# Head of a fused layernorm, linear attention and gated MLP kernel: one warm matmul fewer, an ungated load, one copy on another engine, one tile's statistics moved

## The chip, the cores and the metric

One core of a Trainium2 chip. The metric is device time in microseconds of one execution, the median of five runs. The engines named here are TensorE (PE, with PEld for its weight loads), VectorE (DVE), ScalarE (ACT), GpSimd (POOL) and SyncE (SP, which only issues transfers here). Each of them runs its own list of instructions in order and waits on semaphores for the others.

## What is computed

```python
xn = _layernorm(x)                        # x: 1 x 2048 x 448, bf16
# A: linear attention, 16 heads of 28
qkv = (xn @ wqkv)                         # wqkv: 448 x 1344
pq, pk = phi(q), phi(k)                   # phi(t) = where(t > 0, t + 1, exp(t)) + 1e-6
kv = einsum("bhsd,bhse->bhde", pk, v)
z = einsum("bhsd->bhd", pk)
s = ((pq @ kv) / (pq . z + 1e-6)) @ wo
# B: squared-ReLU MLP with a gate
h = relu(xn @ w1 + b1) ** 2               # w1: 448 x 1792
g = silu(h @ w2 + b2)
return x + s * g
```

All inputs and the output are bfloat16.

## The kernel before

The 2048 tokens are cut into 16 tiles of 128, four tiles to a group. Every tile is loaded token by token (`x_tok`), normalized (`xn`) and transposed (`xT`, features on the partitions), because the matmuls contract over features. The 448 features are three chunks of 128 and one of 64; the last 64 stand twice in `xn` (the "twin" copy, line 496), so that the remainders of two products can run side by side in the two halves of the array.

The kernel is written as a list of operations (`Op`) that a small planner in `Program` puts in order. `add` (line 64) notes what an operation reads and writes. `schedule` (line 87) lays the operations out on an estimated time line and so fixes the order on each engine; TensorE and SyncE keep the order in which the code adds their operations, while the other engines take the ready operation with the least `late`, for which `prio` stands in where it is set. `after` holds an operation back until others are placed. `emit` (line 227) writes each engine's list with the semaphore waits that remain. Every DMA has a semaphore of its own, and each engine one counter.

The change touches the head, in which tiles 0 to 3 go through by hand:

- Loads: tile 0 by SyncE (line 436), tile 1 by ScalarE's queue (437), tiles 2 and 3 by SyncE (439), b1 by ScalarE's queue (440), weights by SyncE. The load of tile 1 names `ones`, a small constant that POOL sets (line 374), as something it reads, so it waits for that memset.
- `warm(n, wide=True)` (line 1036) adds n matmuls of 128x512 on constant data into an unused bank, ahead of all others on TensorE.
- For each tile: statistics (`st`, 458) and their aggregate (`mv`, 459) on VectorE; Ln and Exp (`ln`, 468; `ex`, 472) on ScalarE give the reciprocal standard deviation; VectorE writes xn (`xn`, 481), in two parts for tiles 0 and 1, and the twin (`xd`, 496).
- `pe_transpose` (line 501) adds transposes on TensorE (510) and one copy from PSUM to `xT`, on VectorE (520) or ScalarE (521). Tiles 0 and 1 are transposed in two halves of two chunks: `turn(si, part, eng)`.
- Between them stand the K matmuls of tiles 0 and 1 (621, in the order of lines 1063 to 1069), the transpose of b1 and its copy (1072, 1074), and the matmuls of the first four rows of `w_1` (668, `h_mains`). `rests` (line 587) closes them with the 64-row remainders.
- The order on VectorE and ScalarE is written out by name in lines 1089 to 1096: each name waits in the plan for all names ahead of it in its list.

After the head the groups follow as streams of K, Q and H products (lines 1112 to 1140), then the token sums, the folding of the weights, and the last products with the output (lines 1141 to 1194). None of this is touched. The lists of instructions differ on TensorE, VectorE, ScalarE and POOL only where the section on the change says; SyncE's is the same.

## Time and profile before

| | |
|---|---|
| median of 5 runs | 142.04 us (141.97 to 142.19) |
| the profiled execution | 142.07 us, span 140.8 us |
| TensorE busy | 137.4 us (98%), 1225 matmuls |
| VectorE busy | 92.0 us (65%) |
| ScalarE busy | 78.6 us (56%) |
| GpSimd busy | 22.9 us (16%) |
| warm matmuls, line 1042 | 10, first at 0.84 us |
| landing of x tiles 0, 1 | 2.3 us, 2.5 us after issue |
| landing of x tiles 2 and 3 | 4.1 us after issue |

The span runs from the first to the last instruction that the profiler recorded; the time of the execution holds 1.27 us more. A row of the timeline gives start, duration, engine, line, operation, result and operands, how many instructions it merges, and in brackets the idle time of the engine ahead of it with what ended it. Durations of matmuls include the way through the array, so that neighbours overlap; the pace is read from the distance of their starts.

### The profile page before, as it was taken

Reading aid. Unit: us, or ns where it says so; the run is one execution under the profiler, and the core shown is the slowest. Engines: PE = TensorE matmul, PEld = TensorE weight load, DVE = VectorE, ACT = ScalarE, POOL = GpSimd, SP = SyncE. Lnnn points to the kernel's source line nnn. Section 1 sums busy time; section 2 is a strip of 40 time slices with the busy share of each in tenths; the row PEclk is TensorE's granted clock in tenths of the full one; section 3 lists DMA queues with packets and bytes.
Section 4 is the critical chain, followed back from the end, with each engine's and each line's share of the span. In section 5 each row is a group of like instructions: output and inputs, shape, how many; then the busy total and the mean of one; then the engine's idle time right before and its main releaser. Section 6 shows DMA issues by size and latency. Waiting matters only on the chain.

```text
span 140.8 us, 3056 instructions
## 1 busy us (share of the span) xinstructions
PE 137.4 (98%) x1225; PEld 68.3 (49%) x1225; DVE 92.0 (65%) x224; ACT 78.6 (56%) x152; POOL 22.9 (16%) x38
## 2 busy tenths in 40 slices
PE   7999999999999999999999999999999999999992
PEld 2365444444444444444455445644555555555482
DVE  1989888898878997779959910228936072442753
ACT  3668787978888896979799561523033030300220
POOL 6000000000000000000770000000001419092670
PEclk9999999999999999999999999999999999999999
DMA  4999266999822400000000035980000202122022
GB/s 121 291 304 262 61 169 119 367 294 183 141 41 49 84 14 0 0 19 5 0 0 0 5 81 151 196 167 4 5 0 0 70 0 95 35 69 66 33 96 74
DMA packets 20210, 12.91 MB, mean 92 GB/s; under 512 B 9380, under 2 KB 19812, under 8 KB 20196
## 3 DMA queue, kind: packets, MB, share of 16 engines
q1 hardware_dynamic: 18188, 11.45, 32.7%
q10 hardware_dynamic: 2008, 1.27, 4.0%
q8 instruction: 10, 0.16, 0.5%
q14 instruction: 4, 0.03, 0.1%
HBM read 8.78 MB, written 2.10 MB: 77 GB/s over the span
## 4 chain that ended last, share of the span: by engine, by line
PE 98%; DVE 0%; issue 0%; DVEq 0%
PE pb L935 30%; PE pb L668 30%; PE pb L621 9%; PE pb L1001 8%; PE pb L702 7%; PE pb L652 6%; PE pb L1042 3%; PE pb L708 1%; PE pb L510 1%; PE pb L795 1%; PE pb L756 1%; PE pb L833 0%; DVE xn L971 0%; PE pb L826 0%; DVE xn L980 0%; PE pb L791 0%
## 5 line engine op out<-in xcount | busy, mean ns | idle before, releaser
L668 PE MATMUL pb<-xT,w 64*128 64x512 bf16 (+2 forms) x408 | 51.3, 365 | 0.0
L935 PE MATMUL pb<-w,r 64*128 64x448 bf16 (+3 forms) x378 | 44.7, 343 | 0.0
L677 ACT ACTIVATE r<-pb,b1f 128x512 bf16<-128x512 f32 x56 | 34.9, 689 | 2.8 <-PE pb L668 2.8
L668 PEld LDWEIGHTS pb<-xT,w 64*128 64x128 bf16 (+1 forms) x408 | 22.8, 94 | 22.1 <-ACT r L677 0.5
L935 PEld LDWEIGHTS pb<-w,r 64*128 64x128 bf16 (+1 forms) x378 | 22.7, 95 | 20.0 <-issue 1.2
L911 ACT ACTIVATE gbuf<-gbuf 128x448 bf16<-128x448 bf16 (+1 forms) x16 | 8.7, 565 | 36.0 <-DVE gbuf L946 34.3
L946 DVE TENSOR_TENSOR gbuf<-pb,b2b 128x448 bf16<-128x448 f32 (+1 forms) x16 | 9.3, 609 | 29.2 <-PE pb L935 29.2
L980 POOL TENSOR_TENSOR xn<-xn,x_tok 128x448 bf16<-128x448 bf16 x15 | 15.0, 1031 | 48.8 <-DVE xn L971 48.8
L621 PE MATMUL pb<-w_qkv,xT 64*128 64x512 bf16 (+1 forms) x106 | 17.7, 377 | 0.0
L652 PE MATMUL pb<-xT,w_qkv 64*128 64x512 bf16 x84 | 15.5, 376 | 0.0
L685 DVE TENSOR_TENSOR r<-r 128x512 bf16<-128x512 bf16 x39 | 13.5, 419 | 0.0
L385 POOL MEMSET kvm<- 128x2048 bf16 x1 | 1.8, 1804 | 64.0 <-DVE zb L646 64.0
L458 DVE BATCH_NORM_STATS2 st<-x_tok 128x6 f32<-128x448 bf16 x16 | 9.3, 612 | 3.1 <-DMA x_tok<-in_A_x_dram 3.1
L599 ACT ACTIVATE qk<-pb 128x512 bf16<-128x512 f32 x16 | 8.9, 595 | 4.1 <-PE pb L621 3.6
L609 DVE SCALAR_TENSOR_TENSOR qk<-pb,qk 128x512 bf16<-128x512 f32 x16 | 10.7, 687 | 0.3
L1001 PE MATMUL pb<-msb,pqT 64*128 64x448 bf16 (+3 forms) x93 | 10.9, 343 | 0.0
L971 DVE TENSOR_TENSOR xn<-pb,gbuf 128x448 bf16<-128x448 f32 (+2 forms) x17 | 9.2, 591 | 2.0 <-ACT gbuf L911 1.5
L686 ACT ACTIVATE r<-r 128x512 bf16<-128x512 bf16 x17 | 9.7, 651 | 0.0
L621 PEld LDWEIGHTS pb<-w_qkv,xT 64*128 64x128 bf16 (+1 forms) x106 | 6.6, 94 | 6.3 <-DVE xT L520 0.4
L702 PE MATMUL pb<-qk,xn 128*128 128x448 bf16 x48 | 9.4, 352 | 0.0
L599 ACT ACTIVATE pqT<-pb 128x512 bf16<-128x512 f32 x12 | 6.8, 597 | 3.2 <-PE pb L668 1.6
L652 PEld LDWEIGHTS pb<-xT,w_qkv 64*128 64x128 bf16 x84 | 6.0, 94 | 5.0
(77 smaller groups left out, 98.7 us busy)
## 6 DMA issues: line engine op xcount, KB each, us to landing
out_dram<-xn SPq DMA_DIRECT2D x15, 112.0 KB, 1.7
w<-in_B_w_dram SPq DMA_DIRECT2D x1, 1568.0 KB, 10.0
x_tok<-in_A_x_dram SPq DMA_DIRECT2D x3, 448.0 KB, 3.6
xT<-rows ACTq DMA_DIRECT2D x6, 112.0 KB
w<-in_B_w_dram SPq DMA_DIRECT2D x1, 576.0 KB, 5.2
xT<-rows SPq DMA_DIRECT2D x5, 112.0 KB
w_o<-in_A_wo_dram SPq DMA_DIRECT2D x1, 392.0 KB, 11.2
w_qkv<-in_A_wqkv_dram SPq DMA_DIRECT2D x1, 384.0 KB, 3.4
```

Source lines behind the costliest of these rows:

```text
L599: add("act", lambda e, _: e.activation(out=slot, in_=src(), func=AF.Exp), [buf, "actw"], [tile], 0.6)
L609: lambda e, _: e.scalar_tensor_tensor(out=slot, in0=src(), scalar=1.0 + 1e-6, in1=slot, op0=ALU.add, op1=ALU.max),
L621: return e.matmul(ps(b)[:, 0:512], xT[half[h], c, si * P : (si + 1) * P], w_qkv[half[h], c, 384 : 2 * D], start=start, stop=stop,)
L652: return e.matmul(ps(b)[:, 0:512], w_qkv[half[h], c, m * P : (m + 1) * P], xT[half[h], c, g * 512 : (g + 1) * 512], start=start, stop=stop,)
L668: return e.matmul(ps(b)[:, c0 : c0 + n], w_1[half[h], c, fi * P : (fi + 1) * P], xT[half[h], c, t : t + n], start=start, stop=stop,)
L677: lambda e, _: e.activation(out=slot, in_=ps(b)[:, 0:512], func=AF.Relu, bias=b1f[:, fi : fi + 1]),
L685: return e.tensor_tensor(out=slot, in0=slot, in1=slot, op=ALU.mult)
L686: return e.activation(out=slot, in_=slot, func=AF.Square)
L702: last = e.matmul(ps(b)[:, 0:D], xn[:, si, c * P : (c + 1) * P], pk_of(si), start=(si == 0), stop=(si == NT - 1),)
L935: return e.matmul(ps(b)[:, 0:n], r2[half[h], fi, si * P : (si + 1) * P], w_2[half[h], fi, c], start=start, stop=stop)
L980: eng, lambda e, _: e.tensor_tensor(out=ob, in0=ob, in1=x_tok[:, si, c], op=ALU.add),
L1001: return e.matmul(ps(b)[:, 0:n], q, m, start=start, stop=stop)
```

## The change

Four edits, all in the head:

- nine warm matmuls instead of ten
- the load of x tile 1 no longer names `ones`, so it waits for nothing
- the copy of the second half of tile 1's transpose goes from VectorE to ScalarE, where it stands behind the copy of the first half and ahead of Ln and Exp of tile 2
- on VectorE the statistics and aggregate of tile 3 follow those of tile 2 directly

```diff
-        load_x(1, 2, "act", ["ones"]).prio = -118
+        load_x(1, 2, "act").prio = -118
...
-        warm(10, wide=True)
+        warm(9, wide=True)
...
-        turn(1, 1, "dve")
+        turn(1, 1, "act")
...
-            ("dve", "st0 mv0 st1 mv1 xn00 xn01 xd0 xn10 xn11 xd1 st2 mv2 xT11 st3 mv3 xn2 xd2 xn3 xd3 xT3"),
-            ("act", "ln0 ex0 ln1 ex1 xT00 xT01 xT10 ln2 ex2 b1 ln3 ex3 xT2"),
+            ("dve", "st0 mv0 st1 mv1 xn00 xn01 xd0 xn10 xn11 xd1 st2 mv2 st3 mv3 xn2 xd2 xn3 xd3 xT3"),
+            ("act", "ln0 ex0 ln1 ex1 xT00 xT01 xT10 xT11 ln2 ex2 b1 ln3 ex3 xT2"),
```

In the lists that come out, one of the ten matmuls of line 1042 is gone from TensorE, and its third K matmul of tile 1 waits for ScalarE instead of VectorE. One copy of line 520 is gone from VectorE, and there is one more of line 521 on ScalarE. On POOL the planner now puts the memset of `ones` behind those of `b1r`, `eps5` and `ident`, and the memset of `eps6` behind the selection that makes `ident`. The banks of PSUM are the same.

## The prediction

> **What bounds the kernel now.** First the page: its own time, the chain that ended last, and the tensor engine's share.

> ```profile
> span 140.8 us, 3056 instructions
> ...
> PE 98%; DVE 0%; issue 0%; DVEq 0%
> ```

> The chain is the tensor engine's own work from end to end, and this profiled execution took 142.07 us, 1.27 more than its span. The list of waits says where that engine stands still. For matmuls between 9.7 us and the end it names none; for weight loads it names a few of 0.3 to 0.4 us, which lie under running matmuls. So only the head counts, the first 9.6 us, in which tiles 0 to 3 are normalized and transposed. There the waits name two releasers:

> ```profile
> PEld pb L510 <- DVE xn L481: 1.2, 4, 0.6
> PEld pb L621 <- DVE xT L520: 0.4, 1, 0.4
> ```

> Then the timeline of the head, engine by engine (start, us, what, idle before). TensorE, where PEld is the weight load that shows when a matmul was released:

> ```profile
> 0.84 4.43 PE L1042 MATMUL pb<-const-bfloat16-1.0 128*128 128x512 bf16 x10 [0.84 <-PEq L1210]
> 5.00 0.55 PEld L510 LDWEIGHTS pb<-ident,xn 128*128 128x128 bf16 x4 [0.64 <-DVE xn L481]
> 5.71 0.11 PEld L510 LDWEIGHTS pb<-ident,xn 128*128 128x128 bf16 x2 [0.16 <-DVE xn L481]
> 6.41 1.08 PE L621 MATMUL pb<-w_qkv,xT 128*128 128x512 bf16 x4
> 7.09 0.10 PEld L621 LDWEIGHTS pb<-w_qkv,xT 128*128 128x128 bf16 x1 [0.37 <-DVE xT L520]
> 8.12 0.31 PEld L510 LDWEIGHTS pb<-ident,xn 128*128 128x128 bf16 x4 [0.21 <-DVE xn L481]
> 8.84 0.31 PEld L510 LDWEIGHTS pb<-ident,xn 128*128 128x128 bf16 x4 [0.22 <-DVE xn L481]
> 9.54 0.10 PEld L621 LDWEIGHTS pb<-w_qkv,xT 64*128 64x128 bf16 x2 [0.21 <-issue]
> ```

> VectorE, which works almost without a pause from 3.14 to 9.0:

> ```profile
> 3.14 0.63 DVE L458 BATCH_NORM_STATS2 st<-x_tok 128x6 f32<-128x448 bf16 x1 [3.14 <-DMA x_tok<-in_A_x_dram]
> ...
> 3.90 0.59 DVE L458 BATCH_NORM_STATS2 st<-x_tok 128x6 f32<-128x448 bf16 x1
> ...
> 6.78 0.26 DVE L520 COPY xT<-pb 128x256 bf16<-128x256 bf16 x1
> 6.95 0.62 DVE L458 BATCH_NORM_STATS2 st<-x_tok 128x6 f32<-128x448 bf16 x1
> 7.61 0.18 DVE L459 BATCH_NORM_AGGREGATE mv<-st 128x2 f32<-128x6 f32 x1
> 7.70 0.36 DVE L481 TENSOR_SCALAR xn<-x_tok,mv,rstd 128x448 bf16<-128x448 bf16 x1
> ```

> ScalarE and its queue:

> ```profile
> 0.93 0.40 ACTq L396 DMA_DIRECT2D x_tok<-in_A_x_dram  x1
> ...
> 5.41 1.01 ACT L521 ACTIVATE xT<-pb 128x256 bf16<-128x256 bf16 x3
> 6.90 0.29 ACT L468 ACTIVATE vep<-mv,eps 128x1 f32<-128x1 f32 x1 [0.48 <-DVE mv L459]
> ...
> 7.82 0.29 ACT L468 ACTIVATE vep<-mv,eps 128x1 f32<-128x1 f32 x1
> ```

> To be seen: each transpose waits for VectorE's normalized tile, VectorE's row is set by the landing of x tile 0 at 3.14, and the stalls of the matmuls after 5.85 are small. From the starts of single matmuls: 0.04 before the one released at 7.09, 0.09 and 0.04 around the transposes at 8.12, 0.10 and 0.04 around those at 8.84, 0.31 together. The 0.10 at 9.54 follows the switch to 64-row tiles; later switches (70.5, 95.3) cost the same, so no edit touches it.

> **The change, part by part.** *The tenth warm matmul.* It begins at 4.63 and takes 0.43, so the array is free at 5.06. The weights of the first transpose are in at 5.00, released by xn of tile 0. Without the tenth, that transpose starts at 5.01, 0.05 earlier. It doesn't last: the fifth transpose, at 5.72, waits for tile 1's xn (the row 5.71), which VectorE's order sets, and the K matmuls at 5.85 stand behind it. Bounds 0.00 to 0.05; I take 0.00, since the row 5.71 is the nearest. What the nine do to the clock is the first rival.

> *x tile 1 at once.* Its DMA leaves ScalarE at 0.93 after the memset of `ones`; SyncE's first DMA leaves at 0.81, so it comes forward by at most 0.12. Gain: none. Tile 1's statistics start at 3.90, straight behind tile 0's aggregate, without a wait for data. The b1 transfer behind it on that queue moves too; its reader at 7.32 waits for nothing. On POOL the `ones` memset goes back past three others (0.1 to 0.2 us each) and the memsets of b1r, eps5 and ident come forward a few hundredths; `ident` was ready at 1.73 for a use at 5.00, `ones` is read near 79 us. SyncE's queue is unchanged. Price: tile 1's packets meet tile 0's. Between 1.8 and 2.4 us the queue view has 73 packets, all SyncE's; between 2.4 and 2.8 it has 97 of ScalarE's and 77 of SyncE's at a DMA share of 1. A start that is 0.12 earlier can push tile 0's landing by 0 to 0.12; I take 0.05, since tile 0 had over half its packets through before tile 1's first. All of VectorE's row moves with it.

> [...]

> *xT of tile 1, second half, on ScalarE.* Its transposes end near 6.57. VectorE began the copy at 6.78, behind tile 2's statistics, and ended at 7.04. ScalarE is free at 6.42; it took up its first copy 0.03 after the transposes (5.41), so it starts here at 6.60 and, at 0.38 (first of the three at 5.41), ends at 6.98. The K matmul waiting at 7.09 had its place at 7.06: 0.04 gained. Behind the copy on ScalarE stands tile 2's Ln, at 6.90 now: copies follow each other at 0.31, so it starts between 6.91 and 7.01, Exp 0.32 later, Exp's end 0.20 after that: 7.43 to 7.53, and xn of tile 2 0.04 to 0.08 later (as for tiles 3 and 0): 7.47 to 7.61.

> *Tile 3's statistics moved up.* They start at 6.78 instead of 6.95; the aggregate goes from 7.61 to 7.44 and leaves VectorE free for xn of tile 2 at 7.53 instead of 7.70. With ScalarE's bound that is 7.53 to 7.61, so 0.09 to 0.17 gained; tile 2's transposes come at 8.00 to 8.04 instead of 8.13, since the matmuls before them end no earlier than 8.00. For tile 3 the Ln at 7.82 had waited for the aggregate's end at 7.79. Now that end is 7.62, but the b1 copy (7.58, now 7.54, 0.18 long) is ahead on ScalarE: Ln at 7.65 to 7.75, 0.07 to 0.17 earlier. Exp, xn, the transposes at 8.84 and the matmuls behind them follow by the same amount. These transposes are the head's last wait, so 0.07 to 0.17 goes on to the end; I take the middle, 0.12. Next late is nothing on record: matmuls never wait after 9.7, and the four copies and statistics that follow move along.

> Sum: 0.00 + 0.12 − 0.05 = 0.07 gained. On the profiled execution's 142.07 that gives 142.00; the median of the runs is 0.03 below it, so **141.97**. Ends: 0.17 gained with no delay, 141.87; 0.07 gained with 0.12 of delay, 142.09.

> **Rivals.** *The clock opens late (slower).* Warm matmuls are loaded every 0.43 us; the four of L621 after 6.41 take 0.22 each. The trace's clock record grants full speed from 5.13, 4.29 us after the first warm matmul, and takes it back at 141.66, 3.4 us after the last matmul's end near 138.3. So the gate judges stretches of some 3.4 us. In the one that ended at 5.13 the tensor engine was full; with nine it is idle from 4.63 to 5.01. If that share no longer suffices, the next chance comes near 8.53. Then from 5.85 on: two matmuls 0.86, two transposes 0.21, four matmuls 1.71, to 8.63; from there at full speed, b1 and six matmuls 0.71, transposes and matmuls of tiles 2 and 3 with nothing left to wait for 1.10, the switch 0.10: 10.54 instead of 9.55, less 0.04 for the matmul in which the clock opens. That is 0.95 more, **142.99**. For it: the idle stretch is new, the work after it is short transposes. Against: nine still fill nine tenths of the stretch, and the times of before lie within 0.22 us, so no run there missed its opening, wherever the stretch began. It decides if the K matmuls come 0.43 apart. Its bounds are 0 and, cold until 9.55, some 2.9 (3.2 of work doubled, less 0.31 of stalls).

> [...]

> *The early transfer eats the gain.* Tile 0 lands 0.12 or more late: 142.05 to 142.12. For it: every later start on VectorE hangs on 3.14. Against: over half of tile 0 is through by then.

> *All stalls go.* If Ln of tile 3 slips ahead with the statistics and the copies overlap as well as the first three did, all 0.31 goes: **141.73**. For it: VectorE loses 0.26 of work between 6.0 and 9.0. Against: the b1 copy and its transpose hold ScalarE.

> **How the numbers follow.** My forecast 0.45; late clock 0.27; transfer eats it 0.13; all stalls go 0.13; something else 0.02. Under 0.2% (0.28 us) a measurement here can hardly be told from no change. Faster by more: the case of all stalls and a little besides, 0.15. Slower: the late clock and the rest, 0.29. Within: 0.56. The likeliest case's own range is 141.87 to 142.09. To leave out under 2 in 10 the range has to reach down to the full gain and up through most of the late clock: 141.70 to 143.05.

> **What would show it.** Right: statistics of tile 0 at 3.14 to 3.26; first transpose near 5.0, fifth at 5.7 to 5.8; the copy of tile 1 on ScalarE near 6.6; the K matmul without a stall; tile 2's transposes at 8.0 to 8.1 and the first 64-row matmul at 9.4 to 9.5. Wrong: L621 matmuls at 0.43 each after 5.85, a start of VectorE past 3.3, or Exp of tile 2 later than 7.6.

## The result and the profile after

| | before | changed |
|---|---|---|
| median | 142.16 us (80 runs, 141.97 to 143.28) | 142.39 us (45 runs, 142.04 to 145.0) |
| ratio to before | | 1.0026, 95% interval 1.0016 to 1.0037 |
| profiled execution | 142.07 us, span 140.8 | 142.17 us, span 140.8 |

A little slower, and the table's last row doesn't show it: the two profiled executions have the same span. The difference is in the spread. Each run has a time and a span (first to last recorded instruction). In 134 runs of the kernel before that were taken beside the experiments, the mean time is 142.23, the mean span 140.99, and time less span is never over 1.30. In the 45 runs of the changed kernel the means are 142.64 and 141.18. They include its longest run, 145.0, which the ratio leaves out as over 1.5% above the fastest. So of 0.41 us in the mean, 0.20 lies in the span and 0.21 outside it (0.35, 0.14 and 0.21 without the longest run):

- 9 of the 45 spans are at 141.7 us or more (141.8 to 143.8), against 2 of 134 before.
- 20 of the 45 runs have more than 1.30 us outside the span (1.35 to 2.44).
- The 14 runs that have neither and a span of at most 141.1 average 142.13; the like runs of before 142.16.

So the undisturbed run is where the forecast put it, on the level of before or a little under; what costs is two kinds of disturbance, spans that are longer and time outside the span.

First the page of the changed kernel: its span, the instruction fetches of queue q8, read as the tensor engine's (packets, MB, share), and the chain that ended last.

```profile
span 140.8 us, 3054 instructions
...
q8 instruction: 9, 0.15, 0.4%
...
PE 95%; DMA 2%; DVE 2%; issue 0%; DVEq 0%
```

The chain now begins with the landing of x tile 0 and VectorE's first instructions: the warm matmuls no longer reach up to the first transpose. Two instructions fewer are in the span, a weight load and its matmul, and q8 has 9 packets where the page of before has

```profile
q8 instruction: 10, 0.16, 0.5%
```

Then the head of the changed kernel, TensorE's weight loads (start, us, what, idle before):

```profile
5.17 0.55 PEld L510 LDWEIGHTS pb<-ident,xn 128*128 128x128 bf16 x4 [1.24 <-DVE xn L481]
...
7.18 0.10 PEld L621 LDWEIGHTS pb<-w_qkv,xT 128*128 128x128 bf16 x1 [0.32 <-ACT xT L521]
...
8.81 0.31 PEld L510 LDWEIGHTS pb<-ident,xn 128*128 128x128 bf16 x4 [0.22 <-DVE xn L481]
...
9.52 0.10 PEld L621 LDWEIGHTS pb<-w_qkv,xT 64*128 64x128 bf16 x2 [0.21 <-issue]
```

VectorE:

```profile
3.31 0.63 DVE L458 BATCH_NORM_STATS2 st<-x_tok 128x6 f32<-128x448 bf16 x1 [3.31 <-DMA x_tok<-in_A_x_dram]
...
6.95 0.59 DVE L458 BATCH_NORM_STATS2 st<-x_tok 128x6 f32<-128x448 bf16 x1
7.57 0.18 DVE L459 BATCH_NORM_AGGREGATE mv<-st 128x2 f32<-128x6 f32 x1
7.67 0.37 DVE L481 TENSOR_SCALAR xn<-x_tok,mv,rstd 128x448 bf16<-128x448 bf16 x1
```

and ScalarE:

```profile
0.83 0.40 ACTq L396 DMA_DIRECT2D x_tok<-in_A_x_dram  x1
...
6.75 0.38 ACT L521 ACTIVATE xT<-pb 128x256 bf16<-128x256 bf16 x1 [0.16 <-PE pb L510]
7.06 0.29 ACT L468 ACTIVATE vep<-mv,eps 128x1 f32<-128x1 f32 x1
7.39 0.20 ACT L472 ACTIVATE rstd<-vep 128x1 f32<-128x1 f32 x1
7.67 0.18 ACT L1074 ACTIVATE b1f<-pb 128x14 f32<-128x14 bf16 x1
7.79 0.29 ACT L468 ACTIVATE vep<-mv,eps 128x1 f32<-128x1 f32 x1
```

Tile 0's statistics begin at 3.31 instead of 3.14, 0.17 later, and yet the first 64-row matmul comes at 9.52 instead of 9.54: the copy and the statistics gave 0.2 back on the way.

### The profile page after: what moved, and what is told of

Read it like the earlier page. It is cut to its first block, busy times and chain, and to the rows that moved or that the text cites. A ratio compares the mean times of both kernels' runs of the same rounds, so it can differ in the third digit from the quotient of the medians.

```text
span 140.8 us, 3054 instructions
## 1 busy us (share of the span) xinstructions
PE 136.7 (97%) x1224; PEld 68.3 (49%) x1224; DVE 91.8 (65%) x223; ACT 79.1 (56%) x153; POOL 22.9 (16%) x38
## 3 DMA queue, kind: packets, MB, share of 16 engines
q10 hardware_dynamic: 2008, 1.27, 3.5%
## 4 chain that ended last, share of the span: by engine, by line
PE 95%; DMA 2%; DVE 2%; issue 0%; DVEq 0%
PE pb L935 30%; PE pb L668 30%; PE pb L621 9%; PE pb L1001 8%; PE pb L702 7%; PE pb L652 6%; DMA x_tok<-in_A_x_dram 2%; PE pb L510 1%; PE pb L708 1%; DVE st L458 1%; PE pb L795 1%; PE pb L756 1%; PE pb L833 0%; DVE xn L971 0%; DVE mv L459 0%; PE pb L826 0%
## 5 line engine op out<-in xcount | busy, mean ns | idle before, releaser
L621 PE MATMUL pb<-w_qkv,xT 64*128 64x512 bf16 (+1 forms) x106 | 17.7, 377 | 0.0
L458 DVE BATCH_NORM_STATS2 st<-x_tok 128x6 f32<-128x448 bf16 x16 | 9.3, 610 | 3.8 <-DMA x_tok<-in_A_x_dram 3.8
L621 PEld LDWEIGHTS pb<-w_qkv,xT 64*128 64x128 bf16 (+1 forms) x106 | 6.7, 94 | 6.2 <-ACT xT L521 0.3
```

Of the source, the lines that this page charges most:

```text
L458: add("dve", lambda e, _: e.bn_stats(st6[:, si, :], x_tok[:, si, :]), [("x", si)], [("st", si)], 0.58),
L621: return e.matmul(ps(b)[:, 0:512], xT[half[h], c, si * P : (si + 1) * P], w_qkv[half[h], c, 384 : 2 * D], start=start, stop=stop,)
```

## The experiments

Spans and times are of all runs of a kernel (11 or 12 each), beside the kernel before on the same chip. "Start" is the start of tile 0's statistics and "head" the first 64-row matmul, both of the profiled execution.

| | start | head | mean span (before) | spans ≥ 141.7 | outside > 1.30 |
|---|---|---|---|---|---|
| e1 nine alone | 3.15 | 9.55 | 141.11 (140.94) | 1 of 12 | 7 of 12 |
| e2 ungated alone | 3.30 | 9.70 | 141.22 (140.94) | 1 of 11 | 0 |
| e3 order alone | 3.25 | 9.45 | 140.81 (140.94) | 0 | 0 |
| e4 the change with ten | 3.29 | 9.49 | 140.90 (140.94) | 0 | 0 |
| e5 nine, count kept | 3.20 | 9.60 | 140.86 (140.98) | 0 | 0 |
| e6 ten, a pair less at the end | 3.26 | 9.67 | 140.88 (140.98) | 1 of 12 | 1 of 12 |
| e7 eight, count kept | 3.20 | 11.01 | 141.60 (140.98) | 6 of 12 | 0 |
| e8 order, later gate | 2.87 | 9.67 | 140.72 (140.98) | 0 | 0 |
| e9 the change, count kept | 3.43 | 9.63 | 141.33 (141.02) | 3 of 12 | 0 |
| e10 ten, a pair less early | 3.24 | 9.78 | 141.05 (141.02) | 0 | 4 of 12 |
| e11 nine, a pair less early | 3.17 | 9.83 | 141.58 (141.02) | 5 of 12 | 5 of 12 |
| e12 the change again | 3.20 | 9.41 | 141.24 (141.02) | 2 of 12 | 5 of 12 |
| e13 as e9 | 3.38 | 9.59 | 141.06 (141.00) | 1 of 12 | 0 |
| e14 as e9, gated | 3.10 | 9.31 | 140.89 (141.00) | 0 | 0 |
| e15 as e8 | 3.04 | 9.84 | 140.88 (141.00) | 0 | 0 |

### One part at a time: e1 to e4

```diff
-        warm(10, wide=True)
+        warm(9, wide=True)
```

> The kernel before with nine warm matmuls and nothing else changed. Theory (the clock gate's stretches lie differently in every execution, and nine warm matmuls miss an opening in more of them): two kinds of runs, most with a span within 0.2 us of the kernel before (140.8), some 3 in 10 with 0.3 to 1.6 us more; mean 0.2 to 0.5 us above. Rival (x tile 0's late landing is what costs time): all runs within 0.1 us of the kernel before, no second kind.

```diff
-        load_x(1, 2, "act", ["ones"]).prio = -118
+        load_x(1, 2, "act").prio = -118
```

> The kernel before with x tile 1 issued at once, ten warm matmuls. Theory: tile 0's statistics start 0.1 to 0.2 us later than 3.14, and so the head ends 0.1 to 0.2 us later (first 64-row matmul at 9.65 to 9.75); spans 0.1 to 0.2 us longer in all runs, late openings at most as often as in the kernel before. Rival (the landing at 3.31 was a chance of one run): start of the statistics at 3.14 within 0.05, span unchanged.

```diff
-        turn(1, 1, "dve")
+        turn(1, 1, "act")
...
-            ("dve", "st0 mv0 st1 mv1 xn00 xn01 xd0 xn10 xn11 xd1 st2 mv2 xT11 st3 mv3 xn2 xd2 xn3 xd3 xT3"),
-            ("act", "ln0 ex0 ln1 ex1 xT00 xT01 xT10 ln2 ex2 b1 ln3 ex3 xT2"),
+            ("dve", "st0 mv0 st1 mv1 xn00 xn01 xd0 xn10 xn11 xd1 st2 mv2 st3 mv3 xn2 xd2 xn3 xd3 xT3"),
+            ("act", "ln0 ex0 ln1 ex1 xT00 xT01 xT10 xT11 ln2 ex2 b1 ln3 ex3 xT2"),
```

> The kernel before with only the copy of tile 1's second half on ScalarE and tile 3's statistics moved up. Theory: the head ends 0.15 to 0.22 us earlier (first 64-row matmul at 9.33 to 9.40), span 140.6 to 140.7. Rival (as forecast, 0.07 to 0.17): 9.38 to 9.48. Second rival (gain is lost behind the head): first 64-row matmul earlier and span unchanged.

e4 is the changed kernel with `warm(10, wide=True)`.

> The changed kernel with its tenth warm matmul put back. Theory: the second kind of runs falls back to its share in the kernel before (1 in 10 or fewer), spans within 0.1 us of 140.8, so the whole difference of the means goes. Rival (the loss comes from the transfer or the copy): still 0.2 to 0.4 us above the kernel before in the mean.

Ratios to before: e1 1.0037 (1.0017 to 1.0057), e2 1.0017 (1.0002 to 1.0032), e3 0.9991 (0.9982 to 1.0000), e4 0.9998 (0.9990 to 1.0007). e3 gained less than its theory wanted: the first 64-row matmul at 9.45 and a mean span 0.13 lower are within the rival, the forecast's own 0.07 to 0.17. The tenth matmul makes the loss: with it put back the rest of the change is level. But e1's loss was not the one expected. Only one span of twelve reached 141.7; seven runs had their extra time outside the span, where no theory had put any. And the profiled execution of e1, like that of the changed kernel, had nine fetches of TensorE's instructions, all kernels with ten warm matmuls ten. That made a second theory.

The ungated load costs what its landing shows. e2's queue and VectorE:

```profile
0.83 0.40 ACTq L396 DMA_DIRECT2D x_tok<-in_A_x_dram  x1
```

```profile
3.30 0.63 DVE L458 BATCH_NORM_STATS2 st<-x_tok 128x6 f32<-128x448 bf16 x1 [3.30 <-DMA x_tok<-in_A_x_dram]
```

0.10 us earlier out of the queue, and tile 0's statistics 0.16 later than in the kernel before. Ten of its eleven spans are 141.0 to 141.3, as expected; the eleventh is 142.2.

### Is it the clock or the count of instructions? e5, e6, e7

```diff
-        warm(10, wide=True)
+        warm(9, wide=True)
...
-        add("pe", lambda e, _: e.transpose(b1v(), b1r[:, :], ident[:, :]), ["b1r", "ident"], [bb], 0.1)
+        def b1_turn(e, _):
+            for _i in range(2):
+                last = e.transpose(b1v(), b1r[:, :], ident[:, :])
+            return last
+
+        add("pe", b1_turn, ["b1r", "ident"], [bb], 0.1)
```

> The kernel before with nine warm matmuls, and the transpose of b1 made twice into the same place, so that TensorE has as many instructions as before. Runs with nine warm matmuls so far had up to 1.2 us more outside the span, and their ninth fetch of TensorE's instructions was the last in the span where kernels with ten have a tenth near 137 us. Theory (two instructions fewer move the last fetch behind the span; the clock is another matter): outside the span 1.19 to 1.30 us in all runs, as with ten; spans still with a late kind as in the kernel before with nine alone. Rival (the clock makes both): outside up to 2.5 us in a quarter of the runs.

```diff
-        full(gg(15, cb, True), range(NF + 1))
+        full(gg(15, cb, True))
```

> Ten warm matmuls, and one weight load and matmul fewer at the end of TensorE's list: the last 192 columns of the last tile's gate are left without b2. Theory (fetch): nine fetches in the span and time outside the span between 1.2 and 2.5 us, spans as in the kernel before within 0.1 us, mean time 0.2 to 0.35 us above it. Rival (the clock makes both): outside 1.19 to 1.30 us in all runs, time within 0.1 us of the kernel before.

e7 is e5 with `warm(8, wide=True)` and `range(3)`.

> The kernel before with eight warm matmuls, and the transpose of b1 made three times, so that the count of instructions is as before. Theory (an idle stretch ahead of the transposes makes the clock open one stretch of 3.4 us later in a share of the runs): more and later than with nine: over half of the runs with spans 0.5 to 2 us above 140.8, mean span 0.5 us or more above the kernel before; outside the span 1.19 to 1.30 us. If the profiled execution is a late one, its K matmuls after 5.85 stand 0.43 us apart and the clock record opens past 7 us. Rival (no late clock, only the fetch): spans within 0.2 us of the kernel before.

e5 is at 0.9999 (0.9991 to 1.0008): one useless transpose, and the whole loss of e1 is gone. So most of it came from the count of TensorE's instructions (e1 and e5 ran on different chips; e9 and e12 below repeat the comparison on one). e6 failed as a test of that: one run of twelve had 1.54 us outside the span, the others 1.21 to 1.30, and ten fetches were in the profiled span. The pair it leaves out stands at the end of the list, where it doesn't move the fetch; a pair in the head was needed (e10).

e7 is the clock alone, and there it is seen. Its K matmuls, two and then four in a row:

```profile
5.96 1.06 PE L621 MATMUL pb<-w_qkv,xT 128*128 128x512 bf16 x2
6.81 0.42 PE L510 MATMUL pb<-ident,xn 128*128 128x128 bf16 x2
7.03 1.91 PE L621 MATMUL pb<-w_qkv,xT 128*128 128x512 bf16 x4
...
9.02 0.71 PE L668 MATMUL pb<-xT,w 128*128 128x256 bf16 x5
```

The same rows of e5, with one warm matmul more:

```profile
5.89 0.59 PE L621 MATMUL pb<-w_qkv,xT 128*128 128x512 bf16 x2
6.33 0.28 PE L510 MATMUL pb<-ident,xn 128*128 128x128 bf16 x2
6.44 1.10 PE L621 MATMUL pb<-w_qkv,xT 128*128 128x512 bf16 x4
```

The single starts are 0.43 us apart in e7 (7.03, 7.45, 7.88, 8.31) and 0.22 in e5. The clock record opens at 8.97 in e7 and at 4.74 in e5. The first 64-row matmul is at 11.01 instead of 9.60, and the span at 142.3 instead of 140.9: all of it reaches the end. Six of e7's twelve spans are like this (141.8 to 142.6), the others are as before. The granted clock that the views print is 1.00 even ahead of the record (1.00 for 5 to 9 us in e7, where the matmuls stand 0.43 apart), so the pace of the matmuls has to be read. The ratios are 0.9997 (0.9982 to 1.0012) for e6 and 1.0038 (1.0004 to 1.0072) for e7.

### The place of the last fetch: e9 to e12

e9 is the changed kernel with e5's second transpose of b1.

> The changed kernel with nothing undone, but the transpose of b1 made twice, so that TensorE has as many instructions as before. Theory (the changed kernel's slow runs come from where the last fetch of TensorE's instructions falls, two instructions away): outside the span 1.19 to 1.30 us in all runs, at most one span in ten above 141.15, mean time within 0.1 us of the kernel before, against 0.4 us above it for the changed kernel. Rival (the clock opens late in 3 runs of 10): spans above 141.15 in a quarter or more of the runs, mean 0.2 to 0.4 us above.

```diff
-        mains(k0, (2,), [("xT", 0, 1)])
```

> Ten warm matmuls, and one weight load and matmul fewer in the head: K of tile 0 is left without its third chunk of features. Theory (the place of the fetch counts, whatever shifted it): as with nine, some runs with 0.3 to 1.2 us more outside the span or in it, 3 in 10 or more, and nine fetches in the span of the profiled run. Rival (it takes nine warm matmuls): no such runs, spans at most 0.1 us from the kernel before, and ten fetches.

e11 is e10 with `warm(9, wide=True)`.

> Nine warm matmuls and the head's pair left out as well: four instructions fewer. Theory (the fetch): slow runs as often as with two fewer or more often, up to all of them. Rival (the two fewer instructions are a special place): outside back at 1.19 to 1.30 us in all runs. On the clock alone: as with nine and the count kept, no spans above 141.15.

e12 is the changed kernel itself.

> The changed kernel once more, on the same chip as the three others. Theory: 3 to 5 runs in 10 with 0.3 to 1.6 us more, in the span or outside it; the rest as the kernel before; mean 0.3 to 0.45 us above it. If the profiled execution is one of the slow ones, it shows whether the time lies in the head (clock record opening past 6.2 us) or at the end (the tail after 136 us).

In these runs the time outside the span goes with the head's count of instructions, but for the one run of e6. Over all kernels with 1225 matmuls on TensorE, with ten, nine or eight warm ones, no run of 249 (134 of before, 115 of experiments) has more than 1.30. With a pair less in the head, two in e11, it is 41 of 93, e10 with ten warm matmuls included. The profiled executions agree: in 14 of 17 the span has a tenth fetch, and their time is 1.24 to 1.25 over the span; in the three without one (e1, e12 and the changed kernel) it is 1.39 to 1.51. The expected nine fetches did not show in e10: its profiled execution has ten, and is one of its undisturbed runs with 1.25 outside. The queues between 136 and 139 us, in the kernel before

```profile
q8 instruction: 1, 0.02, 2.0%
q14 instruction: 1, 0.01, 0.7%
```

and in e12:

```profile
q14 instruction: 1, 0.01, 0.9%
```

In the kernel before the last three fetches come after 960, 1088 and 1216 matmuls have started, so one block of 16384 bytes, the size of each of the ten packets, is read as 128 pairs of weight load and matmul, and the queue as TensorE's; the tenth comes 9 matmuls ahead of the end (9 to 18 in the profiles with the count kept). One pair fewer in the head, and in three of four profiles that fetch isn't made within the span any more. That the untraced runs with more time outside lack it too is inferred. The 14 profiles with the tenth fetch in the span have 1.24 to 1.25 us outside it; the three without it have 0.14 to 0.26 more, and no trace shows the runs that have up to 1.2 more. What happens behind the span no trace shows, and why one pair of 1225 decides isn't settled. In e11's profile the tenth fetch is there, but at 140.52, between the last store's issue and its landing, and that landing took 0.8 us longer than the others' 1.7: there the fetch, at 137.34 in the kernel before, came late but inside the span. So with a pair less a long span need not come from the clock.

e9's ratio is 1.0013 (0.9986 to 1.0040), and e12's 1.0038 (1.0013 to 1.0064) on the same chip, where e10 has 1.0016 (0.9999 to 1.0032) and e11 1.0043 (1.0018 to 1.0067). With the count restored the time outside is gone, as expected. The three late spans of e9 (142.5, 142.5, 142.9) were not expected by the theory that wanted all from the fetch.

### Nine with and without the gate: e13 to e15

> The changed kernel with the count of instructions restored, again. Theory (the idle stretch ahead of the transposes, 0.33 us with tile 0 at 3.15 and 0.5 us with tile 0 at 3.3, takes the clock's stretch below what it wants): 2 or 3 of 12 spans at 141.7 or more, mean span 0.15 to 0.4 us above the kernel before. Rival (chance of single chips): none.

e14 is e13 with `["ones"]` put back.

> The same with the load of x tile 1 gated again: nine warm matmuls, the copy and the statistics as in the change, the count of instructions restored. Theory (both edits together make the late clock): at most 1 of 12 spans at 141.7 or more, the others 140.6 to 141.2, mean span 0.1 us below the kernel before. Rival (nine alone makes it): as many as without the gate.

```diff
-        load_x(1, 2, "act", ["ones"]).prio = -118
+        load_x(1, 2, "act", ["ones", "eps5", "eps6"]).prio = -118
```

with e3's edits and ten warm matmuls is e8 and e15.

> Ten warm matmuls, the copy and the statistics as in the change, and x tile 1 held back behind three small memsets instead of one, some 0.05 to 0.1 us later than in the kernel before. Theory (the sooner tile 1's packets come, the later tile 0 lands): tile 0's statistics at 3.05 to 3.15, mean span 140.65 to 140.75, 0.2 us below the kernel before. Rival (landing moves by itself from run to run): no difference to the kernel with the order alone, 140.81.

> The version with ten warm matmuls, the copy and the statistics as in the change and the load of x tile 1 held back behind three memsets, once more. Theory: mean span 0.2 to 0.3 us below the kernel before, no span at 141.7 or more, outside the span 1.19 to 1.30 us. Rival (its first result was luck): within 0.1 us of the kernel before.

Spans of 141.7 us or more, with nine warm matmuls: without the gate 15 of 81 (the changed kernel, e9, e12, e13), with it 1 of 35 (e1, e5, e14). If the gate made no difference, so few with it would come by chance about once in fifty. That leaves out e11, whose profiled execution lost 0.6 us in one wait near 99 us and 0.8 in the last landing; with its 5 of 12 the difference would be no more than chance. Among the kernels with the count kept it is 4 of 24 without the gate (e9, e13) against 0 of 23 with it (e5, e14), once in seventeen. So that nine and the ungated load make the late spans together is likely, not shown. e13, where two or three were expected, has one of twelve and a ratio of 1.0005 (0.9982 to 1.0028); e14, with 0.9994 (0.9981 to 1.0006) and no such span, came as expected.

The load's start sets the landing, in three steps: issued at 0.83 (no gate), statistics at 3.20 to 3.43, mean 3.32 of six profiles; at 0.93, 3.10 to 3.26, mean 3.19 of nine; at 1.00, 2.87 and 3.04. e8's rows:

```profile
1.00 0.40 ACTq L396 DMA_DIRECT2D x_tok<-in_A_x_dram  x1
```

```profile
2.87 0.63 DVE L458 BATCH_NORM_STATS2 st<-x_tok 128x6 f32<-128x448 bf16 x1 [2.87 <-DMA x_tok<-in_A_x_dram]
3.53 0.18 DVE L459 BATCH_NORM_AGGREGATE mv<-st 128x2 f32<-128x6 f32 x1
3.63 0.59 DVE L458 BATCH_NORM_STATS2 st<-x_tok 128x6 f32<-128x448 bf16 x1
```

Tile 1 still comes without a wait. This version has 0.9987 of before (0.9977 to 0.9997) in e8 and 0.9991 (0.9976 to 1.0005) in e15, mean span 0.26 and 0.12 us below. So it is faster in e8, and e15, below its expected 0.2 to 0.3, is not clear of noise; that the later gate adds anything to e3's order (0.9991) is not shown. Its two profiled heads are late ones (9.67, 9.84): by the pace of their K matmuls the clock opened near 6.5 and 6.85, an estimate. So with ten warm matmuls, too, the clock can open late.

## Why the prediction was wrong

The forecast was no change to speak of, with 0.07 us of gain; the kernel is 0.26% slower. The order of terms:

- **The tenth warm matmul, "bounds 0.00 to 0.05; I take 0.00".** This step failed. It looked at the matmul's time on the array and not at its two instructions. With a pair or two less in the head 41 of 93 runs paid 0.1 to 1.2 us outside the span, 0.21 us in the changed kernel's mean, against none of 249 with the count kept. In three profiles the tenth fetch of q8, read as TensorE's last block, was not in the span; how that makes the time stays open. Nothing in the prediction named it, though the page's fetch rows were there to read.
- **The late clock.** A late clock is seen in e7, with eight warm matmuls (K matmuls 0.43 us apart, record open at 8.97), and is the likely cause of the late spans of the changed kernel. It was priced at 0.95 us; the 15 late spans without the gate are 0.9 to 2.0 us over 140.9, one 2.9. What was wrong is what the chance meant. It was put as one case for the whole kernel, with 0.27; it is a share of the runs (9 of 45), because the opening falls at another place in every execution: the record opened between 4.02 and 8.97 in the 13 profiles that have one, at 5.13 in the kernel before and at 4.02 in the changed one, both with the first warm matmul at 0.84. So it adds its share to the mean, about 0.2 us (0.14 without the longest run), and hardly touches the median. The argument against it, that before's five times lay close together "wherever the stretch began", was drawn from too few runs and from a kernel whose stretches were 89% full or more by the estimate above. "Nine tenths of the stretch" for nine counted the gap alone, without the 0.26 among the transposes; with both it is the 75 to 81% above. That the clock judges stretches of 3.4 us was inferred from one end of the record, 141.66 against the last matmul's end at 138.26; in the changed kernel that distance is 2.32 (140.55, 138.23), and it is the lengths of the records that point to 3.41.
- **x tile 1 at once.** Bounds 0 to 0.12, taken 0.05, measured 0.13 in the mean of the profiles (3.32 against 3.19), 0.17 between the two profiles compared. Mis-sized, and its second effect was missed: it widens the gap ahead of the transposes and so, by the estimate above, makes the late clock likelier. The prediction's own sign of being wrong, a start of VectorE past 3.3, came at 3.31.
- **The copy and the statistics.** Bounds 0.07 to 0.17, taken 0.12, measured 0.20: from the start of tile 0's statistics to the first 64-row matmul it is 6.40 to 6.41 without the edits (before, e1, e2, e5, e6) and 6.20 to 6.21 with them (the changed kernel, e3, e4, e9, e12, e13, e14). Mis-sized too. Tile 2's transposes no longer wait at all: their loads follow the matmuls at 8.09, and Ln of tile 3 at 7.79 stands right behind the b1 copy.
- **The sum.** 0.20 less 0.13 is 0.07, the forecast's figure, by two errors that cancel; undisturbed runs are 0.03 below before. Of the other rivals, the early transfer did land tile 0 the 0.12 late that it wanted, and the order edit outweighed it. The stalls did not all go: that of 0.04 before the K matmul and those of 0.09 and 0.04 at tile 2 went but for 0.02, those of 0.10 and 0.04 at 8.81 and the switch stayed.

## What to carry to other kernels

Filler instructions have two sides: the time they fill and the place they take in the instruction stream (here 41 of 93 runs with a pair or two less in the head had more than 1.30 us outside the span, none of 249 with the count kept). When one is added or removed, read where the last fetch of that engine falls against the end of the span, and test with the count held. An event whose place moves from execution to execution, as the clock's opening does here (4.02 to 8.97 us), is a share of the runs, not a case of the kernel: price it as share times cost, and look at the spread of the times, since one profile of each kernel can show the same span. Before a gate that looks needless is taken away, read which transfer would be under way beside the waiting one (here tile 0 landed 0.13 us later when tile 1's load left 0.10 sooner).

## Not expected

- Time outside the span depends on the program: 1.19 to 1.30 us in 249 runs with 1225 matmuls, up to 2.5 with one pair fewer in the head.
- Issuing tile 1's load 0.10 us sooner lands tile 0 0.13 us later, and 0.07 later lands it 0.24 sooner (3.19 to 2.95, two profiles): more than the shift itself.
- Even with ten warm matmuls some executions open the clock past 6.4 us (e8, e10, e15, read from the pace of their K matmuls), and from tile 0's statistics to the first 64-row matmul it is 6.8 us in e8 and e15 instead of 6.2.
